# Three spare blocks of a routed mixture-of-experts kernel moved into a conditional block

## The chip, the cores and the metric

The kernel runs on one core of a Trainium2 chip. The metric is the time of one execution on the device in microseconds (us). Five engines work side by side, each in the order of its own queue: TensorE (PE: matmuls; PEld: its weight loads), VectorE (DVE), ScalarE (ACT), GpSimd (POOL, which also issues the indirect transfers) and SyncE (SP, which issues the other transfers). They wait for one another by semaphores.

## The reference

A causal filter with 7 taps per head, softmax-normalised, runs over x (8 x 3584 tokens of 192 numbers). Each of the 28672 tokens that come out goes to the one of 8 experts whose embedding has the largest cosine with it, and that expert's two-layer net is applied:

```python
    expert_idx = np.argmax(logits, axis=1)
    ...
    for e in range(E):
        mask = expert_idx == e
        ...
        h = np.maximum(x[mask] @ w1[e], 0.0)
        out[mask] = gate_w[mask, None] * (h @ w2[e])
```

w1 is 192 x 1024 and w2 1024 x 192 for each expert. How many tokens an expert gets is known only when the program runs.

## The kernel before, in words

`_Moe.run` (L1338) writes the whole program out, with no branch. The tokens come in 16 chunks of 1792. For a chunk, `mix` (L752) filters and `route` (L796) ranks: each token's expert and its place among that expert's rows. An indirect transfer from GpSimd (`scatter`, L970) writes the token's row into a table in device memory, `rows_d`, in which each expert has a region. `pads` (L981) writes 128 rows behind the last row of each region, and 128 into a dummy region behind all of them, with a token number that is out of range.

The expert work is done in blocks of 512, 256 or 128 rows of one expert. Which expert and which rows a block takes is chosen at run time, the number of blocks and their order are fixed when the program is written. `pick(n, ...)` (L1204) takes as many blocks of n rows as the experts are sure to have; with `last=True` it takes as many blocks of 128 as they could need at most, k = (left + 8 x 127) // 128, where `left` is the number of rows not yet taken. `select` (L1000) computes on VectorE, in some 25 operations on one partition, a table `sel` with the weights' place and the first row of each block. Its `a` (L1015) is a running sum over the experts of the blocks they need, so `a[:, E-1:]` is the number of blocks that are needed. A block beyond that number points to the dummy region (L1036 to L1041).

`last_blocks` (L1329) makes the last four picks and puts their blocks in order: those of 512 and 256 ("mid") and those of 128 ("small") each get fractions, and the list is sorted by these:

```python
        runs = [[((i + o) / (len(g) + o), b) for i, b in enumerate(g)]
                for g, o in ((big, 0.5), (mid, 0.5), (small, 3.0)) if g]
```

Here the picks give no block of 1024, 7 of 512, 8 of 256 and 22 of 128.

`expert` (L1134) does one block of T rows. SyncE fetches rows two blocks ahead: it loads the row's number into a register (L1094), then a transposing transfer (L1101) and one of the token numbers (L1104), into rings of 3 and 6 tiles. VectorE makes a flipped copy (`flip`, L1118) and copies the expert's weights into the one tile `slot` (`copy_w1`, L1062, and `copy_w2`, L1085), each a copy behind a register load (L1071). TensorE multiplies with w1 (L1156, 40 matmuls for T = 128), ScalarE takes the positive part into the tile `hid` (L1160), VectorE its residual (L1162), TensorE multiplies with w2 (L1184, 24 matmuls for each 128 rows), ScalarE scales (L1189), and GpSimd stores 128 rows by an indirect transfer (L1191), which leaves out rows with a token number out of range. The matmuls of the next block may begin while the last ones of a block are still to come.

SyncE's order is the order of the code (`manual_schedule`, L1340 to L1386). In the main part of the program the order on the other engines is set by a scheduler when the program is built: it simulates the engines and gives each the first ready instruction in the order of the code; some are pinned by `_dep` (`behind`, `over`, `under`, L496 to L508) behind the newest matmul, activation or residual. L1402 opens the context in which all this is built; the closing signals and drains of the program bear its number.

Of the kernel before, what the change touches and what calls it, by code (L numbers as in the profile page):

```python
# [15 lines left out]
I32 = mybir.dt.int32  # L16
AF = mybir.ActivationFunctionType
ALU = mybir.AluOpType
# [8 lines left out]
E = 8  # L27
# [23 lines left out]
MARGIN = 30  # L51
KMAX = 32
MORE = 3
EAGER = 4
DIRECT = 2
FLIP = 1.5
# [31 lines left out]
class _Plan:  # L88
# [29 lines left out]
    def run(self):  # L118
        left = self.nodes
        while left:  # L120
            at = [(t + n.pri, k, t) for k, n in enumerate(left)
                  for t in (self.start(n),) if t is not None]
            _, k, t = min(at)
            n = left.pop(k)
            for r in n.takes:
                self.rings[r][1].append(n)
            if n.emit:
                n.emit()
            n.end = self.free[n.engine] = t + n.us
# [10 lines left out]
class _Moe:  # L140
# [859 lines left out]
    def select(self, n, k, last, name, cb, need):  # L1000
        nc, cp = self.nc, self.cp
        sh = n.bit_length() - 1
        one = lambda nm, shape=(1, E), dt=F32: self.lp.tile(
            list(shape), dt, tag="sl_" + nm, name="sl_" + nm)
        av, ai = one("av"), one("ai", dt=I32)
        self.under(nc.vector.tensor_tensor(
            out=av, in0=cb, in1=self.start, op=ALU.subtract).ins)
        nc.vector.tensor_single_scalar(out=ai, in_=av,
                                       scalar=float(n - 1 if last else 0),
                                       op=ALU.add)  # L1010
        nc.vector.tensor_single_scalar(out=ai, in_=ai, scalar=sh,
                                       op=ALU.arith_shift_right)
        nc.vector.tensor_copy(out=av, in_=ai)
        a, ap, bs = one("a"), one("ap"), one("bs")
        nc.vector.tensor_tensor_scan(out=a, data0=self.one8, data1=av,  # L1015
                                     initial=0.0, op0=ALU.mult, op1=ALU.add)
        nc.vector.tensor_tensor(out=ap, in0=a, in1=av, op=ALU.subtract)
        nc.vector.scalar_tensor_tensor(out=bs, in0=ap, scalar=-float(n),
                                       in1=self.start, op0=ALU.mult, op1=ALU.add)
        assert k <= KMAX  # L1020
        jf = self.jf[:, 0:k]
        ge, df = one("ge", (1, k, E + 1)), one("df", (1, k, E))
        nc.vector.memset(ge, 1.0)
        nc.vector.tensor_tensor(
            out=ge[:, :, 1:], in0=a[:].unsqueeze(1).to_broadcast([1, k, E]),
            in1=jf.unsqueeze(2).to_broadcast([1, k, E]), op=ALU.is_le)
        nc.vector.tensor_tensor(out=df, in0=ge[:, :, 0:E], in1=ge[:, :, 1:],
                                op=ALU.subtract)
        nc.vector.tensor_tensor(
            out=df, in0=df, in1=bs[:].unsqueeze(1).to_broadcast([1, k, E]),  # L1030
            op=ALU.mult)
        ro, tm, se = one("ro", (1, k)), one("tm", (1, k)), one("se", (1, k))
        nc.vector.tensor_reduce(out=ro, in_=df, op=ALU.add, axis=AX.X)
        nc.vector.scalar_tensor_tensor(out=ro, in0=jf, scalar=float(n), in1=ro,
                                       op0=ALU.mult, op1=ALU.add)
        if last:  # L1036
            nc.vector.tensor_scalar(out=tm, in0=jf, scalar1=-float(n),
                                    scalar2=float(self.dummy), op0=ALU.mult,
                                    op1=ALU.add)
            nc.vector.tensor_tensor(out=tm, in0=tm, in1=ge[:, :, E], op=ALU.mult)  # L1040
            nc.vector.tensor_tensor(out=ro, in0=ro, in1=tm, op=ALU.add)  # L1041
        nc.vector.tensor_reduce(out=se, in_=ge[:, :, 1:], op=ALU.add, axis=AX.X)
        nc.vector.tensor_scalar(out=se, in0=se, scalar1=float(E - 1),
                                scalar2=float(IMG), op0=ALU.min, op1=ALU.mult)
        sel = cp.tile([1, k, 2], I32, name=name)
        nc.vector.tensor_copy(out=sel[:, :, 0], in_=se)
        nc.vector.tensor_copy(out=sel[:, :, 1], in_=ro)
        if not last:
            t = one("t")
            nc.vector.tensor_scalar(out=t, in0=ap, scalar1=-1.0,  # L1050
                                    scalar2=float(k), op0=ALU.mult, op1=ALU.add)
            nc.vector.tensor_single_scalar(out=t, in_=t, scalar=0.0, op=ALU.max)
            nc.vector.tensor_tensor(out=t, in0=t, in1=av, op=ALU.min)
            nc.vector.scalar_tensor_tensor(
                out=self.start, in0=t, scalar=float(n), in1=self.start,
                op0=ALU.mult, op1=ALU.add)
        for j in range(k):
            for u in range(0, n, 512):
                self.subs.append((sel, j, n, u, need))
# [195 lines left out]
    def head(self, first):  # L1255
# [34 lines left out]
        def more():  # L1290
            self.subs += sum(self.pick(128, first, most=MORE), [])

# [22 lines left out]
    def steer(self, spent):  # L1315
        have, steps = [0.0, 0.0], 0
        for v in self.subs[self.at:]:
            T = min(v[2], 512)
            steps += NFC * T // 512 + T // 128
            for k, t in enumerate(self.slack(512)):  # L1320
# [3 lines left out]
                                 for v, h, s in zip(COST, have, spent)))  # L1324
        self.rate = 3.0 if self.end <= EAGER else min(self.rate, 3.0)
        due = NT * self.end + (E + 1) * (self.end == self.nch)
        self.pace = (due - len(self.scatters)) / max(1.0, steps - MARGIN)

    def last_blocks(self):  # L1329
        big = self.pick(1024)  # L1330
        mid = self.pick(512) + self.pick(256)
        small = self.pick(128, last=True)
        runs = [[((i + o) / (len(g) + o), b) for i, b in enumerate(g)]
                for g, o in ((big, 0.5), (mid, 0.5), (small, 3.0)) if g]
        for _, b in sorted(sum(runs, []), key=lambda v: v[0]):
            self.subs += b

    def run(self):  # L1338
        self.left, self.rate = 0, 1.0
        order = self.tc.manual_schedule(engines={self.nc.sync.engine})  # L1340
        order.__enter__()
        w = self.cp.tile([H, KT], F32, name="cw")
        self.nc.sync.dma_start(out=w, in_=self.weight)
        em = self.op.tile([128, D], F32, tag="y", name="em")[0:E, :]
        self.nc.sync.dma_start(out=em, in_=self.emb)
        tb = self.cp.tile([TP, 1], F32, name="tau_b")
        self.nc.sync.dma_start(out=tb, in_=self.tau.partition_broadcast(TP))
        self.constants()
        self.conv_taps(w)
        self.embeddings(em, tb)  # L1350
        self.onef = self.op.tile([128, D], F32, tag="y", name="onef")[:, 0:128]
        self.nc.gpsimd.memset(self.onef, 1.0)
        first, e = min(PICK), self.nc
        with self.tc.manual_schedule(engines={
                e.tensor.engine, e.vector.engine, e.scalar.engine}):
            self.head(first)
        a, spent = self.dispatch(first), list(DONE)
        self.gated = True
        live, due, done = next(a, None), [0.0, 0.0], False
        while live or self.pend or not done or self.at < len(self.subs):  # L1360
            if self.at < len(self.subs):
                for v in self.expert():
                    self.settle()
                    self.steer(spent)
                    self.due_out = min(SAVED if self.pend else 1.0,
                                       self.due_out + self.pace)
                    due = [min(CAP, d + self.rate * t) for d, t in zip(due, v)]
                    while live and min(due) >= 0.0:
                        if live is WAIT:
                            live = next(a, None)  # L1370
                            if live is WAIT:
                                break
                            continue
                        due = [d - t for d, t in zip(due, live)]
                        spent = [s + t for s, t in zip(spent, live)]
                        live = next(a, None)
            else:
                self.put()
                self.settle()
                self.clk += 0.5  # L1380
                if live:
                    live = next(a, None)
            if not live and not done and not self.pend:
                self.last_blocks()
                done = True
        order.__exit__(None, None, None)  # L1386


@with_exitstack
# [16 lines left out]
```

## Time and profile before

| | us |
|---|---|
| median of 3 runs | 1202.3 |
| lowest, highest | 1198.38, 1203.38 |
| the profiled execution, its own time | 1202.03 |
| its span, first to last instruction | 1200.3 |
| its mean granted TensorE clock | 0.968 of full speed |

The profile is of one execution. Its times count from the first instruction of the span; the execution's own time is 1.73 us longer than the span. An instruction's row gives its start, its duration, its engine, its line, and in brackets how long the engine had been idle and what ended that. A "q" behind an engine's name (POOLq) is its sequencer, the part that handles loads of registers, semaphores and drains. A clock of 1.00 is 2.4 GHz, of 0.5 1.2 GHz.

### The profile page before, as it was taken

To read this page: it belongs to the slowest core of one execution; us is meant where nothing else is said; L and a number is where in the kernel's file an instruction comes from. 1 tells how busy PE (TensorE), PEld (TensorE's weight loads), DVE (VectorE), ACT (ScalarE), POOL (GpSimd) and SP (SyncE) were. 2 spreads that over 40 slices of the span, in tenths; PEclk is the share of its full clock that TensorE was granted. 3 is DMA by queue.
4 is the path that set the end of the run, shared out by engine and by line. 5 is a ranking of instruction groups with operands and counts; after the bars stand their busy time and mean duration, and the time that the engine had idled before them with its cause. 6 is when DMAs were issued, how large, how long until landed. Compare 5 with 4: busy or idle time off the path is not lost. (4 is left out here: it accounts for less than half of the span.)

```text
span 1200.3 us, 29865 instructions
## 1 busy us (share of the span) xinstructions
PE 1129.8 (94%) x10924; PEld 922.8 (77%) x10924; DVE 877.1 (73%) x2337; ACT 597.3 (50%) x1363; POOL 549.7 (46%) x541
## 2 busy tenths in 40 slices
PE   5736999999989999999999999999999999999998
PEld 3623887989879897788976767677776868889997
DVE  5996988797968879858787685754466555567775
ACT  4867856364645636546454563433334343333332
POOL 1282245747635574655765555555542322222222
PEclk9556999999999999999999999999999999999999
DMA  9862355836367575673754836343312212112221
GB/s 266 239 214 49 80 121 129 157 94 151 86 135 148 116 156 113 141 153 75 168 137 105 178 86 114 82 106 81 80 46 58 50 36 55 49 41 48 45 46 25
DMA packets 269188, 127.80 MB, mean 106 GB/s; under 512 B 210494, under 2 KB 259005, under 8 KB 269040
## 3 DMA queue, kind: packets, MB, share of 16 engines
q1 hardware_dynamic: 245216, 79.00, 31.4%
q0 software_dynamic: 23808, 46.87, 14.6%
q8 instruction: 86, 1.41, 0.5%
q14 instruction: 62, 0.51, 0.1%
q10 hardware_dynamic: 16, 0.01, 0.0%
HBM read 38.35 MB, written 47.53 MB: 72 GB/s over the span
## 5 line engine op out<-in xcount | busy, mean ns | idle before, releaser
L1156 PE MATMUL h_ps<-e_xT,slot 128*128 128x256 f16 (+2 forms) x3232 | 503.5, 288 | 7.4 <-DVE slot L1083 5.5
L1184 PE MATMUL o_ps<-slot,hid 128*128 128x192 f16 x5544 | 488.8, 246 | 4.4 <-DVE hid L1162 3.5
L1184 PEld LDWEIGHTS <-hid 128*128 128x128 f16 x5544 | 458.9, 98 | 33.5 <-issue 9.4
L1156 PEld LDWEIGHTS <-slot 128*128 128x128 f16 x4040 | 352.2, 98 | 159.8 <-issue 11.6
L1191 POOL DMA_INDIRECT out_dram<-y,e_mt x231 | 254.5, 1102 | 451.2 <-ACT y L1189 424.7
L1162 DVE SCALAR_TENSOR_TENSOR hid<-h_ps,hid 128x512 f16<-128x512 f32 x462 | 313.3, 686 | 114.8 <-ACT hid L1160 112.1
L1160 ACT ACTIVATE hid<-h_ps 128x512 f16<-128x512 f32 x462 | 272.8, 597 | 203.4 <-PE h_ps L1156 197.0
L971 POOL DMA_INDIRECT rows_d<-rows,di x256 | 278.6, 1088 | 144.1 <-PE h_ps L1156 40.8
L1189 ACT ACTIVATE y<-o_ps,g 128x192 f32<-128x192 f32 x231 | 96.5, 421 | 310.4 <-PE o_ps L1184 278.1
L1156 PE MATMUL h_ps<-e_xf,slot 128*128 128x256 f16 (+2 forms) x808 | 222.3, 288 | 0.0
L1086 DVE COPY slot<-res 128x3074 f16 x101 | 99.1, 981 | 130.8 <-PE o_ps L1184 130.4
L1083 DVE COPY slot<-res 128x3072 f16 (+1 forms) x125 | 100.4, 803 | 0.4 <-issue 0.2
L760 PE MATMUL conv_ps<-xt,band 128*112 128x384 f32 x208 | 83.9, 495 | 0.2 <-ACT xt L765 0.2
L765 ACT COPY xt<-conv_ps 112x384 f32<-112x384 f32 x104 | 49.4, 480 | 29.5 <-PE conv_ps L760 28.8
L1123 DVE COPY e_xf<-e_xT 64x256 f16<-64x256 f16 (+2 forms) x202 | 47.1, 233 | 21.8 <-DMA e_xT<-rows_d 17.6
L772 ACT ACTIVATE sq<-xt 112x192 f32<-112x192 f32 x156 | 55.5, 361 | 2.0 <-DVE sq L776 0.9
L807 ACT CAST rows<-xt 112x768 f16<-112x768 f32 x56 | 46.2, 833 | 15.9 <-DVE xt L805 8.0
L805 DVE TENSOR_TENSOR xt<-xt,x_p_s 112x768 f32<-112x768 f32 x56 | 51.7, 951 | 0.2
L842 PEld LDWEIGHTS <-xT 128*112 128x112 f16 x672 | 44.0, 131 | 9.2 <-DMA xT<-rows 4.4
L842 PE MATMUL lg_ps<-ma,xT 128*112 128x16 f16 x448 | 43.6, 193 | 3.9 <-DMA xT<-rows 3.8
L809 DVE TENSOR_TENSOR rows<-xt,rows 112x512 f16<-112x512 f32 x56 | 38.4, 685 | 6.5 <-ACT rows L807 6.4
L842 PE MATMUL lg_ps<-mb,xT 128*112 128x16 f16 x224 | 37.7, 196 | 0.3 <-ACT xT L837 0.3
(211 smaller groups left out, 643.7 us busy)
## 6 DMA issues: line engine op xcount, KB each, us to landing
xt<-in_dram SPq DMA_DIRECT2D x42, 384.0 KB
res<-in_dram SPq DMA_DIRECT2D x6, 768.0 KB
rows_d<-rows,di POOLq DMA_INDIRECT x256
out_dram<-y,e_mt POOLq DMA_INDIRECT x231
xT<-rows SPq DMA_TRANSPOSE x208
res<-in_dram SPq DMA_DIRECT2D x6, 512.0 KB
xt<-in_dram SPq DMA_DIRECT2D x2, 1536.0 KB
xt<-in_dram SPq DMA_DIRECT2D x2, 1440.0 KB
```

The lines of the kernel that those rows point to most:

```text
L760: i = nc.tensor.matmul(out=ps, lhsT=self.band[:, h, :], rhs=xt[:, :, h * G:(h + 1) * G], start=True, stop=True).ins
L772: self.over(nc.scalar.activation(out=sq, in_=xc[:, t, :], func=AF.Square, accum_out=n2[:, t:t + 1]).ins)
L842: i = nc.tensor.matmul(out=lg[:, g * GX + a, :], lhsT=xT[:, a, k, :], rhs=self.mb if k == 1 else self.ma, start=(k == 0), stop=(k == 2)).ins
L971: i = self.nc.gpsimd.indirect_dma_start(out=self.rows_d[:, :], out_offset=bass.IndirectOffsetOnAxis(ap=idx, axis=0), in_=src, in_offset=No ...
L1083: self.under(nc.vector.tensor_copy(out=o, in_=v).ins)
L1086: self.nc.vector.tensor_copy(out=self.slot[:, W2:], in_=self.res2[:, bass.ds(self.we, IMG)])
L1156: self.mm = nc.tensor.matmul(out=ps[:, c, :], lhsT=w1(o, b + c), rhs=xk[k], start=(i == 0), stop=(i == 4)).ins
L1160: self.step = nc.scalar.activation(out=hh[:, b:b + m, :], in_=ps, func=AF.Relu).ins
L1162: self.low = nc.vector.scalar_tensor_tensor(out=hl[:, b:b + m, :], in0=ps, scalar=0.0, in1=hh[:, b:b + m, :], op0=ALU.max, op1=ALU.subtrac ...
L1184: self.mm = nc.tensor.matmul(out=o, lhsT=h[:, c, q], rhs=w2[:, c, k:k + D], start=(n == 0), stop=(n == 3 * NFC - 1)).ins
L1189: self.step = nc.scalar.activation(out=y, in_=o, func=AF.Copy, scale=g[:, a:a + 1]).ins
L1191: i = nc.gpsimd.indirect_dma_start(out=self.out[:, :], out_offset=bass.IndirectOffsetOnAxis(ap=mt[:, a, 0:1], axis=0), in_=y, in_offset=No ...
```

## The change

The count of needed blocks yields `over_k` = max(0, needed + 3 - k), a number in a tile of one element: how many of the last three small blocks have rows. The last three are taken out of the list of small blocks before the order is made. Behind everything else, all engines load `over_k` into a register, and the three blocks stand in a conditional block that is entered when it is not 0. `self.step = self.low = self.mm = None` takes away the instructions behind which those of the conditional block would be pinned.

```diff
+SPARE = 3
...
         if last:
+            self.over_k = cp.tile([1, 1], I32, name="over_k")
+            nc.vector.tensor_scalar(out=self.over_k, in0=a[:, E - 1:],
+                                    scalar1=float(SPARE - k), scalar2=0.0,
+                                    op0=ALU.add, op1=ALU.max)
...
         small = self.pick(128, last=True)
+        small, self.spare = small[:-SPARE], sum(small[-SPARE:], [])
...
         order.__exit__(None, None, None)
+        more = self.nc.values_load(self.over_k[0:1, 0:1], min_val=0, max_val=SPARE)
+        self.step = self.low = self.mm = None
+        with self.tc.If(more != 0):
+            self.subs += self.spare
+            while self.at < len(self.subs):
+                for _ in self.expert():
+                    pass
```

## Rows read from the trace of the kernel before

**Rows 1.** Busy times of the page, then windows: busy us (instructions) by engine, clock, DMA.

```profile
PE 1129.8 (94%) x10924; PEld 922.8 (77%) x10924; DVE 877.1 (73%) x2337; ACT 597.3 (50%) x1363; POOL 549.7 (46%) x541
...
core 0: us, PE busy (x) PEld busy (x) DVE busy (x) ACT busy (x) POOL busy (x), PEclk, DMA share, GB/s
900.00:940.00 40.00, 40.00 (x321) 27.85 (x319) 24.17 (x68) 16.01 (x30) 10.59 (x11) 1.00 0.23 54
940.00:1000.00 60.00, 60.00 (x623) 48.47 (x622) 33.38 (x62) 21.90 (x44) 15.23 (x15) 1.00 0.21 48
1000.00:1140.00 140.00, 140.00 (x1592) 123.11 (x1590) 94.34 (x181) 53.07 (x101) 34.84 (x33) 1.00 0.20 46
1140.00:1194.40 54.40, 54.39 (x697) 52.63 (x694) 40.02 (x77) 20.42 (x39) 13.99 (x13) 1.00 0.18 39
905.00:915.00 10.00, 10.00 (x81) 6.94 (x80) 7.91 (x23) 4.23 (x8) 0.35 (x1) 1.00 0.29 57
```

**Rows 2.** Timeline, last 30 us: start us, duration us, engine, line, operation, tiles, count.

```profile
1173.19 0.39 PE L1156 MATMUL h_ps<-e_xT,slot 128*128 128x128 f16 x4
...
1177.08 0.39 PE L1156 MATMUL h_ps<-e_xT,slot 128*128 128x128 f16 x4
...
1177.44 0.39 DVE L1123 COPY e_xf<-e_xT 64x128 f16<-64x128 f16 x2
...
1177.83 0.42 ACT L1189 ACTIVATE y<-o_ps,g 128x192 f32<-128x192 f32 x1 [1.61 <-DVE e_xf L1123]
...
1181.36 1.04 PE L1156 MATMUL h_ps<-e_xT,slot 128*128 128x256 f16 x8
...
1182.23 0.49 PE L1184 MATMUL o_ps<-slot,hid 128*128 128x192 f16 x4
...
1182.56 1.04 PE L1156 MATMUL h_ps<-e_xT,slot 128*128 128x256 f16 x8
1182.76 0.97 DVE L1086 COPY slot<-res 128x3074 f16 x1 [0.44 <-PE o_ps L1184]
1182.76 0.42 ACT L1189 ACTIVATE y<-o_ps,g 128x192 f32<-128x192 f32 x1 [2.29 <-PE o_ps L1184]
...
1190.01 0.39 PE L1156 MATMUL h_ps<-e_xT,slot 128*128 128x128 f16 x4
...
1192.25 2.14 PE L1184 MATMUL o_ps<-slot,hid 128*128 128x192 f16 x24
...
1194.43 0.42 ACT L1189 ACTIVATE y<-o_ps,g 128x192 f32<-128x192 f32 x1 [1.38 <-PE o_ps L1184]
1195.12 0.97 POOL L1191 DMA_INDIRECT out_dram<-y,e_mt  x1 [2.48 <-ACT y L1189]
```

**Rows 3.** DMA queue of GpSimd's stores (packets, MB) in 1166.5:1170, 1178.4:1189, 1191.6:1195, 1195:1200.3.

```profile
q0 software_dynamic: 48, 0.05, 4.3%
...
q0 software_dynamic: 96, 0.00, 0.5%
...
q0 software_dynamic: 96, 0.20, 17.5%
...
q0 software_dynamic: 48, 0.00, 0.5%
```

**Rows 4.** Line 1402, the closing: ns min/median/max, first and last start in us.

```profile
L1402 SPq EVENT_SEMAPHORE  x12: 17/28/28, 1194.2 to 1200.3; - x12
...
L1402 POOLq DRAIN  x3: 40/107/4633, 1194.9 to 1200.1; - x3
L1402 SPq DRAIN  x3: 7/7/13, 1197.8 to 1199.8; - x3
...
L1402 PEldq EVENT_SEMAPHORE  x2: 51/51/51, 1199.7 to 1200.3; - x2
```

**Rows 5.** Lines 1094 and 1071 (register loads, from 900 us on), 1006, and the selection's ends.

```profile
L1094 SPq TENSOR_LOAD <-sel x37: 269/273/285, 899.9 to 1171.3; - x37
L1094 SPq FUSED_REGOPS  x37: 159/159/159, 900.2 to 1171.6; - x37
L1094 SPq SEQ_ASSERT  x37: 18/18/18, 900.4 to 1171.8; - x37
...
L1071 DVEq TENSOR_LOAD <-sel x37: 302/310/321, 911.4 to 1186.9; - x37
...
L1006 DVE TENSOR_TENSOR sl_av<-cb,start x14: 146/147/155, 74.5 to 903.2; 1x8 f32<-1x8 f32 x14
...
903.22 0.15 DVE L1006 TENSOR_TENSOR sl_av<-cb,start 1x8 f32<-1x8 f32 x1
...
909.99 0.15 DVE L1047 CAST sel<-sl_ro 1x22 int32<-1x22 f32 x1
```

**Rows 6.** The page's DMA queues: packets, MB, share of 16 engines' span; TensorE's instructions.

```profile
q8 instruction: 86, 1.41, 0.5%
```

## The prediction

> **What bounds the kernel now.** I read first the busy times and the windows by stage. TensorE is busy 94% of the span, VectorE 73%, and from 900 us on TensorE's busy time equals the length of the window at granted clock 1.00, up to its last matmul at 1194.4 us [rows 1]. So the last 290 us are pure TensorE time: what leaves TensorE's queue there leaves the span, and what leaves VectorE or ScalarE does not.
>
> Next the timeline of TensorE in the last 27 us [rows 2]. The order of the last blocks reads: 128 rows from 1173.19, 128 from 1177.08, 256 from 1181.36, 128 from 1190.01, last matmul over at 1192.25 + 2.14 = 1194.39. The list that makes this order (the fractions in `last_blocks`) has 22 small blocks with numbers 0 to 21 and 15 middle ones; these four are small 19, small 20, the last middle block and small 21. The three small ones are what the diff takes.
>
> Then whether these three carry rows at all [rows 3]. Each block ends in one indirect store of 128 rows. The evictions for small 19 and 20 come at 1177.83 and 1182.76, and the stores after them moved 96 packets with 0.00 MB in 1178.4 to 1189; the one after small 21 moved 48 packets with 0.00 MB. The two stores of the middle block moved 0.20 MB with as many packets, and small 18, ahead of these, moved 0.05 MB, half a block. So exactly three blocks store nothing, and they are the last three. The reference's inputs say the same: with the rows counted by expert, the eight experts need 19 small blocks and the list has room for 22. The new count is max(0, 19 + 3 - 22) = 0: the block isn't entered.
>
> Last the closing [rows 4]. After the last matmul 5.9 us remain (1200.3 - 1194.4). GpSimd issues the last store at 1195.12, but its DRAIN, begun at 1194.9, takes 4.63 us, to 1199.5; the other engines wait for it in the closing, SyncE, which waits for the landings of the stores, goes on from 1197.8. The last 0.8 us are the engines' signals.
>
> **The change part by part.** The sum is made against the profiled execution, 1202.03 us, which is its span of 1200.3 plus 1.73 around it. It stands 0.3 us below the median of 1202.3.
>
> *Three blocks leave TensorE.* From the first matmul of small 19 (1173.19) to the first one of the middle block that follows small 20 unmixed (1182.56) pass 9.37 us, of which 0.87 are eight matmuls of the middle block taken early (1181.36 to 1182.23). So two blocks cost 8.50, one 4.25. Checked by parts: 40 matmuls from 1190.01 to 1192.25 and 24 from there to 1194.39 make 4.38 with the end of the last one in it. 3 x 4.25 = 12.75 [rows 2]. After the change the order ends small 16, middle, small 17, middle, small 18: again a 128 behind a 256, as now, so the end has the same shape. I take **-12.7**.
>
> With them go, per block, two weight copies, a flip and two residual passes on VectorE (it is busy 40.02 of 54.40 us there, so it stays behind TensorE), and one row fetch, one metadata fetch, one store. None of these is on the path [rows 1]: 0. Fewer SyncE fetches can only come earlier; the ring of three still sets them.
>
> *One VectorE instruction in the last selection,* a 1x1 operation: a like one takes 0.15 us [rows 5]. The selection runs from 903 to 910 us [rows 5]; from 905 to 915 TensorE is busy 10.00 of 10.00 and VectorE 7.91 [rows 1]. Hidden by TensorE's queue of prepared blocks: 0. Without that cover 0.15.
>
> *The count is loaded on all five engines.* SyncE's own load of this kind is a TENSOR_LOAD of 0.27, register work of 0.16 and an assert of 0.02; VectorE's load takes 0.31 [rows 5]. The five run side by side: 0.5 us once. Where it stands in each queue is not written down in the kernel: only SyncE's order is. At the end of TensorE's queue it is issued while matmuls still run. If it is moved forward to just behind the selection, TensorE's queue (all later matmuls) would wait for VectorE there, at most the 6.9 us of the selection (903.22 to 909.99 and its last 0.15) [rows 5], and ScalarE's likewise. I take the end of the queue, since TensorE has no idle time into which a later instruction would be moved: 0 exposed, bounds 0 and 6.9.
>
> *The branch and what replaces the skipped work.* No row shows a branch. Behind the waiting branch of each engine stands only the closing, and the closing waits for all. Low end: nothing, since GpSimd's DRAIN covers everything the other four do in 1194.4 to 1199.5, and its own load could lie beside the work that it drains. A gain is excluded: nothing of the closing is removed. High end: one closing more, 5.9 us, if the engines have to join, with GpSimd drained, before they may jump [rows 4]. Semaphores that the skipped block would have raised must be raised in another way; such an instruction takes 0.02 to 0.05 us in the closing, where SyncE has twelve of them [rows 4]: 12 x 0.03 is 0.4, and 0.5 with the gaps between. Of the two ends I take the low one with what these rows add to it, 0.5 of load and 0.5 of semaphores on GpSimd's queue, **+1.0**, since a join needs an instruction that the engines have no reason for before the closing.
>
> Sum: 1202.0 - 12.7 + 1.0 = **1190.3 us**, a gain of 1.0%.
>
> One rule speaks against the change. First what the trace shows: TensorE's instructions come over a queue of their own, 86 packets and 1.41 MB for 2 x 10924 of them [rows 6], so 16 KB and some 254 instructions a packet; the three blocks are 3 x 128 = 384 instructions, one and a half packets, and the engine has never left their order. The Trainium skill (Runtime: NRT & Kernel Launch, "Instruction fetch mechanics") says that a taken branch to a place outside the instructions at hand makes the engine wait until they are fetched; that is rival A, and by it the sum would be 1194.1. The Trainium skill (Advanced Engine Details and Errata, "Control Flow Timing") gives a compare-and-branch 108 ns, and an estimate from that alone puts the sum at 1189.4. No run here shows either yet.
>
> **The rivals.**
>
> *A, the jump stalls for instructions.* A packet of TensorE's instructions took 0.5% x 16 x 1200.3 / 86 = 1.1 us [rows 1, 6]; from a request to data that has landed the nearest row is the last store, issued at 1195.12 and waited for by SyncE until 1197.8, 2.7 us [rows 2, 4]. Together 3.8 us. On TensorE or VectorE that ends by 1194.4 + 3.8 = 1198.2, under GpSimd's drain; it shows only on GpSimd, whose skipped part is three stores. Time if it shows: 1190.3 + 3.8 = **1194.1**. Against it: so short a part; for it: the size of TensorE's.
>
> *B, a full join ahead of the branch.* All engines wait until GpSimd is drained and the last store has landed, and a second closing follows: +5.9 in place of the 1.0 of semaphores and load, about **1195.7**. For it: the skipped block overwrites tiles that are in use until the very end. Against it: a wait for those uses needs the last matmul and eviction (1194.85), not the drain.
>
> *C, slower: joins on both sides of the block.* If the conditional is built as drain and join before the jump, again after it, and again in the closing's own order, each at the price of 5.9, it decides from 12.7 / 5.9 = 2.2 closings on: with three, 1202.0 - 12.7 + 17.7 = **1207.0**. Against it: most of the 5.9 is one drain, which finds little the second time.
>
> *D, it doesn't do what it says: the block is entered.* Then the 12.7 returns behind the branch, with the first block's fetch (2.7, as under A), its flip (0.39) and the load of its row (0.45) uncovered [rows 2, 5], and the 1.0: 1202.0 + 1.0 + 3.5 = **1206.5**. Against it: the 0.00 MB of three stores.
>
> **How the numbers follow.** Chances: forecast 0.66, A 0.12, B 0.13, C 0.05, D 0.04. About 0.5%, 6.0 us, is what a measurement of this kernel can tell from no change, so the bound for faster is 1196.3. Forecast and A lie clear of it; B is 0.6 us inside, and I give 0.06 of its 0.13 to faster and 0.07 to no change. C and D make 0.09 on the slower side, of which 0.01 could be milder forms that end within the bound. Faster 0.84, same 0.08, slower 0.08. The range: the low end is the full 12.75 with all else hidden, 1189.3, less what runs of one kernel differ by (three of before lie between 1198.4 and 1203.4, half that spread being 2.5): 1187.0. The high end takes in A and B: 1196.5. An early load that held TensorE for the whole 6.9 us of its bound would end at 1197.2, just outside it.
>
> **What would show it.** In the changed profile: 228 stores where there are 231, 10924 - 192 = 10732 matmuls, TensorE still without gaps from 900 us on and its last matmul near 1194.4 - 12.7 = 1181.7; the order 256, 128, 256, 128 at the end; GpSimd's closing DRAIN of about the same length. The stretch from last matmul to end should be 5.9 to 7 us; at about 10 it is rival A, at 11 to 12 rival B, at over 18 C. A gap of TensorE near 905 to 910 us would show the early load. The prediction is wrong if TensorE's last matmul hardly moves, or if the closing grows by more than 6.

## The result and the profile after

The changed kernel takes 1186.28 us (4 runs, 1184.81 to 1188.07) against 1202.17 of the kernel before in the same session: a ratio of 0.9877, 95% interval 0.9859 to 0.9896. Taken once more, 1187.19 us (5 runs, 1185.87 to 1188.83) against 1200.65 (23 runs, 1197.75 to 1202.92): 0.9885, interval 0.9871 to 0.9900. The forecast was 1190.3, the range 1187.0 to 1196.5: the way and the size are right, and the gain, 15.9 and 13.5 us, is 4.2 and 1.8 us larger than the 11.7 of the sum. The first median lies 0.7 us under the range, the second just inside it. The first runs of four experiments below come from a session in which the kernel before needed 1276.8 us, and they are compared with that alone.

The profiled execution took 1184.81 us, with a span of 1183.1. Its busy times, and the windows of its last stage, which answer to [rows 1]:

```profile
PE 1118.7 (95%) x10732; PEld 911.5 (77%) x10732; DVE 866.3 (73%) x2314; ACT 592.3 (50%) x1354; POOL 546.5 (46%) x538
...
core 0: us, PE busy (x) PEld busy (x) DVE busy (x) ACT busy (x) POOL busy (x), PEclk, DMA share, GB/s
900.00:940.00 40.00, 40.00 (x309) 27.02 (x308) 23.00 (x49) 16.77 (x31) 7.96 (x8) 1.00 0.22 51
940.00:1000.00 60.00, 60.00 (x633) 49.07 (x631) 32.84 (x62) 20.11 (x40) 15.07 (x15) 1.00 0.21 51
1000.00:1140.00 140.00, 140.00 (x1587) 124.28 (x1586) 93.89 (x177) 54.29 (x104) 36.00 (x34) 1.00 0.19 44
1140.00:1180.00 40.00, 37.40 (x479) 36.19 (x476) 27.01 (x51) 14.26 (x27) 10.62 (x10) 1.00 0.19 41
```

TensorE has the 192 matmuls less and still no gap up to its last matmul, which ends at 1177.40. The timeline of the changed kernel, at the last selection and in the last 20 us (lines behind the diff are up to 13 higher, so 1189 is the second layer's matmul and 1196 the store):

```profile
899.07 0.15 DVE L1007 TENSOR_TENSOR sl_av<-cb,start 1x8 f32<-1x8 f32 x1
...
1160.48 0.39 PE L1161 MATMUL h_ps<-e_xT,slot 128*128 128x128 f16 x4
...
1165.57 1.04 PE L1161 MATMUL h_ps<-e_xT,slot 128*128 128x256 f16 x8
...
1173.02 0.39 PE L1161 MATMUL h_ps<-e_xT,slot 128*128 128x128 f16 x4
...
1175.26 2.14 PE L1189 MATMUL o_ps<-slot,hid 128*128 128x192 f16 x24
...
1177.44 0.42 ACT L1194 ACTIVATE y<-o_ps,g 128x192 f32<-128x192 f32 x1 [1.38 <-PE o_ps L1189]
1178.13 0.97 POOL L1196 DMA_INDIRECT out_dram<-y,e_mt  x1 [2.48 <-ACT y L1194]
```

The order ends 128, 256, 128, and from the start of the last 128 to the end of its last matmul the two kernels agree: 1173.02 to 1177.40 here, 1190.01 to 1194.39 in [rows 2]. The last selection began at 903.22 in [rows 5] and begins at 899.07 here. From it to the last matmul pass 291.17 us before and 278.33 after, 12.84 less. The other 4.15 us of this pair of profiles were gained ahead of the selection, where the change has nothing; the first experiment is about them.

The conditional, by line (1393 the load of the count, 1395 the branch and what stands in place of the skipped block), then the closing at line 1415:

```profile
L1393 SPq TENSOR_LOAD <-over_k x1: 283/283/283, 902.1 to 902.1; - x1
...
L1393 POOLq TENSOR_LOAD <-over_k x1: 504/504/504, 1173.7 to 1173.7; - x1
...
L1393 PEldq TENSOR_LOAD <-over_k x1: 488/488/488, 1176.8 to 1176.8; - x1
...
L1395 SPq COMPARE_BRANCH  x1: 58/58/58, 1158.5 to 1158.5; - x1
L1395 POOLq COMPARE_BRANCH  x1: 45/45/45, 1174.3 to 1174.3; - x1
...
L1395 POOLq INC_SWDGE_SEM  x1: 924/924/924, 1174.5 to 1174.5; - x1
L1395 DVEq COMPARE_BRANCH  x1: 72/72/72, 1176.6 to 1176.6; - x1
L1395 PEldq COMPARE_BRANCH  x1: 3447/3447/3447, 1177.4 to 1177.4; - x1
L1395 ACTq COMPARE_BRANCH  x1: 45/45/45, 1178.0 to 1178.0; - x1
...
L1415 POOLq DRAIN  x3: 40/112/4387, 1177.9 to 1182.8; - x3
```

Here lies what no row of before could show. There is no join: SyncE passes its branch 16 us ahead of the next engine, GpSimd ahead of its last two stores (1174.68 and 1178.13). Four of the five branches take 0.05 to 0.07 us. TensorE's takes 3.45, from 1177.43 to 1180.88. And GpSimd's drain begins at 1177.9 and lasts 4.39, to 1182.3: the jump ends 1.4 us before the cover does. From the last matmul to the end pass 5.7 us, where [rows 4] give 5.9.

### The profile page after: what moved, and what is told of

The parts are those of the page before. It is cut to its first block, busy times and chain, and to the rows that moved or that the text cites. A ratio compares the mean times of both kernels' runs of the same rounds, so it can differ in the third digit from the quotient of the medians.

```text
span 1183.1 us, 29407 instructions
## 1 busy us (share of the span) xinstructions
PE 1118.7 (95%) x10732; PEld 911.5 (77%) x10732; DVE 866.3 (73%) x2314; ACT 592.3 (50%) x1354; POOL 546.5 (46%) x538
## 5 line engine op out<-in xcount | busy, mean ns | idle before, releaser
L1161 PE MATMUL h_ps<-e_xT,slot 128*128 128x256 f16 (+2 forms) x3136 | 496.5, 290 | 5.1 <-DVE slot L1088 4.8
L1189 PE MATMUL o_ps<-slot,hid 128*128 128x192 f16 x5472 | 481.8, 246 | 3.3 <-DVE hid L1167 2.2
L1189 PEld LDWEIGHTS <-hid 128*128 128x128 f16 x5472 | 453.7, 98 | 31.8 <-issue 9.4
L1161 PEld LDWEIGHTS <-slot 128*128 128x128 f16 x3920 | 345.5, 98 | 157.9 <-issue 10.9
L1167 DVE SCALAR_TENSOR_TENSOR hid<-h_ps,hid 128x512 f16<-128x512 f32 x456 | 309.2, 686 | 112.9 <-ACT hid L1165 110.7
L1165 ACT ACTIVATE hid<-h_ps 128x512 f16<-128x512 f32 x456 | 269.1, 597 | 199.3 <-PE h_ps L1161 192.1
L1161 PE MATMUL h_ps<-e_xf,slot 128*128 128x256 f16 (+2 forms) x784 | 217.8, 291 | 0.0
L1091 DVE COPY slot<-res 128x3074 f16 x98 | 96.6, 986 | 131.2 <-PE o_ps L1189 125.8
L1088 DVE COPY slot<-res 128x3072 f16 (+1 forms) x119 | 96.4, 810 | 1.2 <-issue 0.6
L808 ACT CAST rows<-xt 112x768 f16<-112x768 f32 x56 | 46.1, 832 | 11.7 <-DVE xt L806 4.5
```

What stands on the lines that cost most here:

```text
L1088: self.under(nc.vector.tensor_copy(out=o, in_=v).ins)
L1091: self.nc.vector.tensor_copy(out=self.slot[:, W2:], in_=self.res2[:, bass.ds(self.we, IMG)])
L1161: self.mm = nc.tensor.matmul(out=ps[:, c, :], lhsT=w1(o, b + c), rhs=xk[k], start=(i == 0), stop=(i == 4)).ins
L1165: self.step = nc.scalar.activation(out=hh[:, b:b + m, :], in_=ps, func=AF.Relu).ins
L1167: self.low = nc.vector.scalar_tensor_tensor(out=hl[:, b:b + m, :], in0=ps, scalar=0.0, in1=hh[:, b:b + m, :], op0=ALU.max, op1=ALU.subtrac ...
L1189: self.mm = nc.tensor.matmul(out=o, lhsT=h[:, c, q], rhs=w2[:, c, k:k + D], start=(n == 0), stop=(n == 3 * NFC - 1)).ins
```

## The experiments

For each profile below the same two stretches are taken from its rows: from the first operation of the last selection (as 899.07 above) to the end of the last matmul (as 1175.26 + 2.14), and from there to the end of the span.

| kernel | last selection | last matmul ends | between | closing |
|---|---|---|---|---|
| before | 903.22 | 1194.39 | 291.17 | 5.9 |
| before, again | 901.49 | 1192.66 | 291.17 | 5.9 |
| changed | 899.07 | 1177.40 | 278.33 | 5.7 |
| changed, again | 903.10 | 1181.41 | 278.31 | 5.7 |
| blocks left out, no conditional | 901.69 | 1180.01 | 278.32 | 5.7 |
| conditional alone | 902.79 | 1193.96 | 291.17 | 5.9 |
| one block in the conditional | 902.04 | 1188.93 | 286.89 | 6.0 |
| two conditionals | 901.82 | 1180.15 | 278.33 | 8.2 |
| block entered | 904.97 | 1198.23 | 293.26 | 7.3 |
| conditional 4 blocks earlier | 899.88 | 1185.33 | 285.45 | 5.7 |

**Both kernels once more.** Is the lead of 4.15 us at the last selection the change's? Nothing is edited.

> The kernel before, unchanged, once more. Theory 1 (the three blocks are worth 12.7 us, and the further lead of 4.1 us that the changed kernel's profile has at the last selection is what single executions differ by): ratio 1.000 within 0.003, and in this profile the last selection begins anywhere between 898 and 904 us (903.2 and 899.1 in the two profiles so far). Theory 2 (the further lead belongs to the change): the last selection begins within 1 us of 903.2 again.

> The changed kernel, unchanged, once more. Theory 1: with more runs the gain comes back towards 12.9 us (12.7 of TensorE and a closing 0.2 shorter), a ratio of 0.989 to 0.990, and the last selection may begin anywhere between 898 and 904 us. Theory 2: 16 us, a ratio of 0.987, and the last selection within 1 us of 899.1.

Measured: 0.9996 (0.9985 to 1.0006) and 0.9885 (0.9871 to 0.9900). The last selection began at 901.49 in the kernel before and at 903.10 in the changed one: this time the changed kernel is the later one. Over the ten profiles it begins anywhere from 899.07 to 904.97, whatever the kernel. Theory 2 falls. What stays the same to 0.02 us is what comes behind: 291.17 against 278.31 to 278.33.

**The three blocks left out, without a conditional.** What the blocks are worth free of any price:

```diff
-        small = self.pick(128, last=True)
+        small = self.pick(128, last=True)[:-3]
```

> The three last small blocks left out altogether: no count, no load, no conditional. They hold no rows with these inputs. This is what the blocks are worth without any price. Theory 1 (the conditional's whole price lies under GpSimd's closing drain): the same time as the changed kernel within 1 us, last matmul 12.7 us earlier in relation to the last selection, closing 5.7 to 5.9 us. Rival A (TensorE's jump of 3.4 us is paid): 3.4 us faster than the changed kernel. Theory 2 (the layout with the new tile brings 3 to 4 us): 3 to 4 us slower than the changed kernel, at 1189.

Measured: 1187.41 us, ratio 0.9889 (0.9874 to 0.9903). The changed kernel, with all its loads, branches and the jump of 3.4 us, is as fast as the one that has none of them, within intervals of 1.7 us to either side, and the two stretches agree to 0.02 and 0.1 us. So the conditional's whole price is hidden, GpSimd's part beside the last block's matmuls and TensorE's jump under the closing.

**The conditional alone.** All 22 blocks stay in the order, the conditional holds the last three once more:

```diff
-        small, self.spare = small[:-SPARE], sum(small[-SPARE:], [])
+        self.spare = sum(small[-SPARE:], [])
```

> The conditional alone: all 22 small blocks stay in the order, and behind everything stands the conditional block with the last three once more, skipped as in the changed kernel. Theory 1: ratio 1.000 within 0.0015, the closing 5.7 to 6.0 us, TensorE's COMPARE_BRANCH again about 3.4 us and over before GpSimd's drain. Rival A: 3.4 us slower, 1.003. Theory 2: 3 to 4 us faster, 0.997.

Measured: 1.0005 (0.9993 to 1.0016), 291.17 us to the last matmul and a closing of 5.9, both those of the kernel before. The same answer from the other side. TensorE's branch took 2.2 us here, where about 3.4 had been expected:

```profile
L1395 PEldq COMPARE_BRANCH  x1: 2218/2218/2218, 1194.0 to 1194.0; - x1
```

**One block in the conditional.** A price per block needs a second point, and a jump over 128 instructions of TensorE in place of 384 tells what the 3.4 us come from:

```diff
-SPARE = 3
+SPARE = 1
```

> SPARE = 1: one block in the conditional, 21 in the order. The step of TensorE at 4.25 us a block: 4.3 us faster than the kernel before, ratio 0.9965, and 4.3 us less from the last selection to the last matmul. If the gain hung on taking all three (the order of the end, the join), it would be near 0 or near 13. On the jump: if TensorE's 3.4 us come from the length of what is jumped over (384 instructions then, 128 here), its COMPARE_BRANCH is here as short as on the other engines, below 0.1 us; if every taken branch of TensorE costs that, 2 to 3.6 us again.

> SPARE = 1 again, since the session before ran all kernels 6% slower and its intervals were some 3 us to either side. One block at 4.25 us: 4.3 us faster than the kernel before, ratio 0.9965; 283.65 us from TensorE's matmul 7744 to the last one where the kernel before has 287.9. TensorE's COMPARE_BRANCH below 0.5 us again, if the length of the jump decides (0.37 us in the first look); 2 us and more if that was chance.

Measured first: 0.9964 (0.9936 to 0.9993). Second: 0.9969 (0.9957 to 0.9980), and 286.89 us, 4.28 less than before. Three blocks gave 12.84 = 3 x 4.28: the term is linear. TensorE's branch:

```profile
L1395 PEldq COMPARE_BRANCH  x1: 367/367/367, 1189.0 to 1189.0; - x1
```

0.37 us, both times. But the conditional below, which stands earlier, skips 384 instructions in 0.45, so length alone isn't it. What tells the cases apart is TensorE's own instruction queue (q8 in [rows 6]). In the changed kernel, in the stretch of the jump, 1177.43 to 1180.88:

```profile
q8 instruction: 1, 0.02, 1.9%
```

One packet of 16 KB came while the branch lasted. In the jumps of 0.37 and 0.45 us none came; the last one ahead of them had begun 2.8 us or more before they ended. In the one of 2.2 us none came inside it, but in the window that begins 0.5 us earlier one did, so it was under way already. When the window is narrowed, the packet begins at 1178.45 in the changed kernel, 2.4 us ahead of the branch's end. The seven long branches take 2.2 to 3.7 us, but each ends 2.4 to 2.8 us after its packet began: the length goes with the packet. These rows agree with the rule that the prediction set against the change (the Trainium skill, Runtime: NRT & Kernel Launch, "Instruction fetch mechanics"), by which a jump to a place not yet at hand waits for its packet. No run changed only what is at hand, so that the packet is the cause is argued from these times.

**Two conditionals, one behind the other.** If the drain of 4.4 us is what hides a jump, a second jump must come out from under it:

```diff
         with self.tc.If(more != 0):
             self.subs += self.spare
             while self.at < len(self.subs):
                 for _ in self.expert():
                     pass
+        with self.tc.If(more != 0):
+            self.subs += self.spare
+            while self.at < len(self.subs):
+                for _ in self.expert():
+                    pass
```

> The changed kernel with a second conditional behind the first, of the same three blocks and the same condition, both skipped: the price doubled. If GpSimd's closing drain hides the first jump (it ends 4.9 us after the last matmul), a second jump of 2.2 to 3.6 us on TensorE ends 4.4 to 7.2 us after the last matmul: 0 to 2.5 us slower than the changed kernel, and the last engine to come to the closing is TensorE. If GpSimd's 0.9 us semaphore step is what counts, 1 us slower. If each conditional brings a join (rival B), about 6 us slower.

> Two conditionals again. From the first look: jumps of 3.4 and 3.2 us one behind the other on TensorE and a closing of 8.0 us. So 2.3 us over the changed kernel's closing of 5.7, ratio to the kernel before 0.9905 where the changed kernel has 0.9885. If only the first look was like that: the changed kernel's time.

Measured first: 0.9895 (0.9846 to 0.9944). Second: 0.9909 (0.9895 to 0.9924), 1189.97 us, 2.8 over the changed kernel, with the same 278.33 to the last matmul and a closing of 8.2 in place of 5.7. TensorE's two branches and the drains of the closing:

```profile
L1395 PEldq COMPARE_BRANCH  x1: 3747/3747/3747, 1180.2 to 1180.2; - x1
...
L1400 PEldq COMPARE_BRANCH  x1: 2975/2975/2975, 1184.1 to 1184.1; - x1
...
L1420 POOLq DRAIN  x3: 40/113/3320, 1181.9 to 1188.0; - x3
...
L1420 PEldq DRAIN  x2: 8/8/8, 1187.4 to 1187.8; - x2
```

GpSimd is drained at 1181.9 + 3.3 = 1185.2. TensorE comes out of its second jump at 1184.1 + 3.0 = 1187.1, and the closing signals follow it. The last to come is now TensorE, by 1.9 us. A join per conditional, rival B, would have cost 5.9 each.

**The block entered.** With the condition turned round the three blocks without rows run behind the branch, which is nearly what an execution pays that has rows for them (its stores would move bytes, which was not tried):

```diff
-        with self.tc.If(more != 0):
+        with self.tc.If(more == 0):
```

> The condition turned round (entered when the count is 0), so that the three blocks without rows run behind the branch: what the conditional costs in an execution that needs it. Rival D's sum: 3 x 4.25 and a start of 3.5 us, and no jump over the block: 16 us above the changed kernel, 1203 to 1207. If the fetches run ahead of the branch as SyncE's early branch suggests, the start is hidden and it is 12.7 to 14 us above, 1200 to 1202.

> The block entered, again. Three blocks at 4.25 us, a gap of TensorE at the branch of 1 to 2 us, and a closing of 7.2 us in place of 5.7 (first look): 14.5 to 16.5 us over the changed kernel, so 1.0 to 3 us over the kernel before, ratio 1.001 to 1.0025. Rival D's sum would be 1206.5 against 1202.0: 1.0037.

Measured first: 0.9990 (0.9957 to 1.0023), which tells nothing. Second: 1.0033 (1.0020 to 1.0046), 1205.87 us, 4.0 us over the kernel before by the ratio (2.4 to 5.5 by its interval). It lies at rival D's price and over what was expected after the first run. The table splits the profile's 3.5: 2.1 us up to the last matmul, 1.4 in the closing. Most of the 2.1 is a start afresh behind the branch, seen on TensorE; the 1.4 is seen on GpSimd, in its last two stores and its drain:

```profile
1184.08 0.62 PE L1161 MATMUL h_ps<-e_xT,slot 128*128 128x128 f16 x8 [0.79 <-DVE slot L1088]
1185.37 0.22 PE L1161 MATMUL h_ps<-e_xf,slot 128*128 128x128 f16 x1 [0.67 <-DVE e_xf L1128]
...
1198.96 0.97 POOL L1196 DMA_INDIRECT out_dram<-y,e_mt  x1 [2.91 <-ACT y L1194]
1200.23 0.98 POOL L1196 DMA_INDIRECT out_dram<-y,e_mt  x1 [0.30 <-issue]
...
L1415 POOLq DRAIN  x3: 40/113/5116, 1199.5 to 1205.2; - x3
```

The weights of the first block and its flipped rows are late by 0.8 and 0.7 us: VectorE passes its branch at 1182.5 and copies and flips only behind it. That is 1.5 of the 2.1; the other 0.6 was traced to no single wait. At the end two stores stand close together: the last store of the main part has its place in GpSimd's queue behind the conditional, so it is issued after those of the block, and the drain ends at 1199.5 + 5.1 = 1204.6, 6.4 us after the last matmul, where it is 5.1 in [rows 4].

**The conditional four blocks earlier.** The same work, without the closing as cover: the last four blocks are taken out of the list and written behind the conditional.

```diff
         for _, b in sorted(sum(runs, []), key=lambda v: v[0]):
             self.subs += b
+        self.tail = self.subs[-TAIL:]
+        del self.subs[-TAIL:]
...
+        self.step = self.low = self.mm = None
+        self.subs += self.tail
+        while self.at < len(self.subs):
+            for _ in self.expert():
+                pass
```

> The same conditional block, skipped too, but four blocks (256, 128, 256, 128 rows) ahead of the end instead of behind everything: the same work, without the cover of the closing. If the price is real and only hidden at the end, TensorE shows a gap there of its jump (2.2 to 3.6 us) and of what has to start afresh behind it, 3 to 9 us over the changed kernel. If a skipped conditional costs next to nothing wherever it stands, within 1 us of the changed kernel.

> The skipped conditional four blocks ahead of the end, again. First look: jump 0.45 us, but the row fetch behind the branch is issued only when the other engines have passed theirs, and TensorE stands 4.5 us. If that is the price of a place inside the stream: 4 to 7 us over the changed kernel, ratio 0.992 to 0.9945. If the gap belonged to the slow session alone: within 1 us of the changed kernel.

Measured first: 0.9921 (0.9893 to 0.9949). Second: 0.9942 (0.9929 to 0.9955), 1194.14 us: 6.9 over the changed kernel, and 7.1 by the table (285.45 - 278.33). Two waits of SyncE's queue in the second profile, for the signals that stand at the branch of VectorE and of TensorE (line 1107 is the row fetch; us in total, times, longest), then windows at the gap and behind it, with the columns of [rows 1]:

```profile
SPq L1107 <- DVEq L1398: 3.4, 1, 3.4
SPq L1107 <- PEq L1398: 1.1, 1, 1.1
```

```profile
1153.05:1157.42 4.37, 0.00 (x2) 0.03 (x2) 2.18 (x4) 0.42 (x1) 1.81 (x1) 0.85 0.41 75
1157.42:1160.00 2.58, 2.58 (x13) 1.84 (x14) 0.33 (x2) 0.00 (x0) 0.00 (x0) 0.50 0.47 92
1160.00:1165.00 5.00, 5.00 (x36) 3.98 (x35) 1.67 (x3) 2.14 (x4) 0.00 (x0) 0.71 0.10 12
1165.00:1170.00 5.00, 5.00 (x73) 5.00 (x71) 3.47 (x7) 1.36 (x4) 1.12 (x1) 1.00 0.09 20
```

The jump is short here, 0.45 us. The price is another: SyncE is past its branch long before, but its next fetch waits until VectorE and TensorE have passed theirs, and TensorE stands idle for 4.37 us until the rows have landed. Then it runs at a granted clock of 0.50 and 0.71, that is partly at 1.2 GHz, and full again from 1165 on. The slow stretch loses 0.50 x 2.58 + 0.29 x 5.00 = 2.7 us, and 4.4 + 2.7 = 7.1 is the whole difference. No run has the same split without a conditional; it is the two waits at line 1398 that tie the gap to the branch. At the end of the program both cost nothing, as nothing is left to fetch or to multiply.

## Why the prediction was right, point by point

- **What bounds.** Right. What left TensorE's queue left the time, one for one: 12.84 us between the same two places. Three blocks at the 4.25 of the rows are 12.75 of it, which leaves 0.1 for anything else, VectorE's 23 instructions less among it.
- **Three blocks leave TensorE, -12.7.** Right: -12.84, and -4.28 for one block, where the rows had given 4.25.
- **The instruction in the selection, and the loads.** Right, in part by chance. On TensorE, VectorE, ScalarE and GpSimd the loads stand at the end of the queue, as taken. SyncE's queue was held to be in the order of the code, but its load stands at 902.1, in the middle of the selection and 256 us ahead of its branch. That this cost nothing was no part of the reasoning; nothing was lost by it, since the time from the selection to the last matmul holds no delay beyond the no-conditional kernel's 278.32.
- **The branch and what replaces the work, +1.0.** This term failed in its size: it is 0 within what can be measured. By the closings the conditional alone adds nothing to 5.9; its ratio, 1.0005 (0.9993 to 1.0016), by itself leaves room for -0.8 to 1.9 us. The step said that 0.5 of load and 0.5 of semaphores would stand on GpSimd's queue behind everything. They are there (0.50 and 0.92), but GpSimd reaches its branch while the last block is still multiplied, and its last store comes behind them. The low end of the bounds was the right one, and for the reason given there: the drain covers what the others do.
- **The closing.** It was taken as unchanged and is 0.2 us shorter, by GpSimd's drain: 4.63 us in [rows 4], 4.39 after. The drain is 4.63 in the profiles of the kernels whose last store has no valid row (before, conditional alone, one block in the conditional) and 4.38 to 4.39 where the last store is that of small 18, with half its rows (changed, blocks left out, conditional four blocks earlier). That the rows are the cause wasn't tried by itself.
- **Where the rest of the difference is.** The sum was made against one execution of 1202.03. Over 23 runs the kernel before takes 1200.65, 1.4 less. 1200.65 - 12.84 - 0.2 = 1187.6, against 1187.19 measured. The first four runs of the changed kernel were on the fast side by another 0.9. The range's low end allowed for the scatter, but from a starting point that was itself high; its own sum, 1189.3 - 2.5, gives 1186.8 and not 1187.0, still above the first median.
- **Rival A** had the mechanism and nearly its size, 3.8 us said and 3.0 to 3.7 measured where a packet had to come, and its own objection held: it falls on TensorE, under GpSimd's drain, and GpSimd's own jump over its three stores took 0.05, so the 1194.1 did not come. The experiment with two conditionals shows the drain as the cover. The Trainium skill (Advanced Engine Details and Errata, "Control Flow Timing") gives 108 ns for a compare-and-branch; the four engines that weren't held up took 45 to 72 ns, so the measurement differs.
- **Rivals B and C** fall: five engines pass their branches between 1158.5 and 1178.0, each in its own time. B's price by its own terms is 1202.0 - 12.7 + 5.9 = 1195.2, where the prediction has 1195.7; with it B lies 1.1 us inside the bound for faster and not 0.6, and the range holds either.
- **Rival D** didn't happen, but its price was tried: 4.5 us over the kernel before was said, 4.0 (2.4 to 5.5) measured. It is made up otherwise than said: the start takes 2.1 in place of 3.5, and the late store adds 1.4 where 1.0 was put for load and semaphores.

## What to carry to other kernels

Padding blocks in a kernel bound by TensorE cost their matmuls, here 4.28 us for 128 rows, and a skipped conditional block behind everything else gives that back whole, as long as a drain of the last store covers the jump. The same block four blocks earlier takes half of it back, by the fetch that waits behind the branch and by the clock after the gap. An execution that enters the block pays 4.0 us over the kernel without the change, so how often that happens decides: from 13.5 gained and 4.0 lost, an estimate is that the change pays while fewer than three in four executions enter it. A difference of a few us should be read between two fixed places of the profile, since here the start of the program differs by up to 6 us from one execution to the next.

## What the runs showed that was not expected

- GpSimd has one instruction in place of the skipped indirect stores, INC_SWDGE_SEM, that takes 0.92 us (0.81 to 0.98 in the profiles with one or three stores skipped), where the closing's semaphores take 0.02 to 0.05.
- TensorE's jump took 0.37 and 0.45 us (twice each), 2.2 us, and 3.0 to 3.7 us (six times) in the profiles: a factor of ten for the same instruction.
- After 4.4 us without a matmul, TensorE was granted half the clock for the next stretch, and that cost another 2.7 us.
